# Where three short steps stand in a sketched attention and gated feed-forward kernel: two token differences and one set of key sums

## The chip, the core and the metric

The kernel runs on one core of a Trainium2 chip. The metric is the device time of one launch in microseconds. Five engines work side by side and meet through semaphores: TensorE (PE in the profile; its weight loads are listed as PEld), VectorE (DVE), ScalarE (ACT), GpSimd (POOL) and SyncE (SP), which here issues transfers. Each takes its instructions in the order of the program.

## The reference, cut to what matters

There are 4 batches, 4 heads, 1088 tokens and a head width of 32. Two 8 x 32 matrices sketch each query and key, and all products of the two sketches make 64 features:

```python
def phi(x):                       # 8 + 8 sketches -> 64 features
    a = np.einsum('rd,bhsd->bhsr', S1, x)
    b = np.einsum('rd,bhsd->bhsr', S2, x)
    return np.einsum('bhsi,bhsj->bhsij', a, b).reshape(*x.shape[:-1], 64)
q_p, k_p = phi(q), phi(k)
kv  = np.einsum('bhsf,bhsd->bhfd', k_p, v)
z   = np.sum(k_p, axis=2)
num = np.einsum('bhsf,bhfd->bhsd', q_p, kv)
den = np.einsum('bhsf,bhf->bhs', q_p, z)[..., None] + 1e-06
x   = (num / den)                 # then (batch, token, head*32): 4352 x 128
g   = x @ w_gate                  # 128 -> 1536
out = (g / (1 + np.exp(-g)) * (x @ w_val)) @ w_out    # 1536 -> 128
```

All is float32 at the interface.

## The kernel before, in words

**Tiling.** The tokens of batch 0 form three blocks of 384, 384 and 320 tokens, and all later tokens form seven blocks of 480, the last of 384 (`blocks`; `line` lists the later ones, so `line[0]` is the first later block and `line[2]` the third). The hidden width of 1536 is 12 chunks of 128. One unit of work is one chunk of one block: gate and value product, SiLU, product, and some units later the projection by `w_out` (`down`, L1045, matmul on L1066) into an accumulator.

**Split products.** Later blocks are computed by `cut_unit` (L965) from operands that are split in parts. For a block of tokens `x`, `cut_tokens` (L867) makes `x1`, the token values scaled by a factor just under one (ScalarE, L875), `x0 = x - x1` (L876) and, in a second step of the generator, the token difference `xd = x1 - 4096 x0` (VectorE, L880). The weights have parts `w1`, `wb`, `wd` likewise. A unit's first matmul (L974) multiplies `wd` by `xd`; ScalarE copies it, scaled, to `sums` (L978); two more matmuls (L984, L985) multiply `w1` by `x1` and `wb` by `x0`, and VectorE adds them into `sums` (L986), which frees the bank of these two. GpSimd then makes the hidden values (L997). Up to step 19 only the value product is split and the gate product is a plain one (L976); from step 20 on both are. A bank is one of eight in PSUM; each product takes the bank that has been left alone longest.

**Attention.** The attention of batches 1 to 3 is the generator `attentions` (L608). It is advanced a part at a time between the units (`parts_of`, L1230), and at a part marked "pe" it stops until `group` (L1237) lets it go on, at steps 4, 6, 20, 22 and 40. For a batch: transposes of the keys; their sketches (`key_products`, L343, matmuls on L347, in two pieces that go to two banks; copies on ScalarE, L583); the features `phk` in four products on VectorE (`features`, L702, instruction on L370); sums of these over the nine groups of tokens in five instructions on GpSimd (`feature_sums`, L536, L540), whose result is `zs`; then, in `values` (L709), 36 value products (`key_values`, L377, matmuls on L381) and 4 key-sum products of `zs` with ones (L713), both into one bank, `kv`. `fold` (L590) folds the key sums into the third set of sketch weights, `spread_out` (L718) turns `kv` and spreads it by small transfers, and `query_step` (L737) makes the query features, beginning with a product `dot` (L741) and a sum `den` (L744). `numerators` (L766) multiplies the two and writes the tokens of the batch, `xT`.

**Order.** The scheduler is set to keep the order written out. Around the change it is this. After batch 0's units a loop (L1323) runs the projections that remain, three at a time. Once `numerators(1, ...)` has been issued (`begun`), the same loop starts `cut_tokens(HEAD, nc.vector)` for the first later block, one step of the generator in each pass, with parts of attention between. Then comes the main loop over 84 units (`y`). At the end of its step `y`, after the parts of attention, it takes the steps of other blocks' `cut_tokens` that `token_steps` (L1342) names for `y`; GpSimd makes `x0` there. The third later block begins at `y` = 24.

Of the kernel before, what the change touches and what calls it, by code (L numbers as in the profile page):

```python
# [19 lines left out]
def kernel(  # L20
# [28 lines left out]
    nc = tc.nc  # L49
# [7 lines left out]
    NC = (NX + 3) // 4  # L57
    F = R * R
    NCH = Dff // P
# [38 lines left out]
    def touch(*which):  # L98
        for i in which:
            clock[0] += 1  # L100
            used[i] = clock[0]

    def hold(*tags):
        for t in tags:
            held.update((place[t], place[t] + 1) if t in "ab" else (place[t],))

    def release(*tags):
        for t in tags:
            banks = (place[t], place[t] + 1) if t in "ab" else (place[t],)
            held.difference_update(banks)  # L110
            touch(*banks)
# [19 lines left out]
    def wide(tag):  # L131
        i = place[tag]
        touch(i, i + 1)
        return PS[:, i : i + 2, :]
# [160 lines left out]
    def run(*gens):  # L295
        for g in gens:
            for _ in g:
                pass
# [78 lines left out]
    def key_values(kv, phk, c0, c1, order=range(NC)):  # L377

        for c in range(c0, c1):
            for h in range(H):  # L380
                nc.tensor.matmul(  # L381
                    kv[32 * h : 32 * h + 32, 0:F],
                    vld[:, h, c, :],
                    phk[:, c, h, :, :].rearrange("p i j -> p (i j)"),
                    start=(c == order[0]),
                    stop=(c == order[-1]),
                )
# [172 lines left out]
    def turn_keys(b):  # L560

        for c in kpieces:
            turn_k(*c)
            if c[1] == NC and b + 1 < B:
                load_k(b + 1)
            yield

    def turn_queries(b):

        for x0, x1 in ((0, 4 * kpieces[0][1]), (4 * kpieces[0][1], 4 * NC)):  # L570
            nc.vector.transpose(out=qT[:, x0:x1, :], in_=qld[:, x0:x1, :])
            if x1 == 4 * NC and b + 1 < B:
                load_q(b + 1)
            yield
# [15 lines left out]
    def fold(kv):  # L590

        t = apool.tile([P, R, R], FP32, tag="fold", name="fold")
        w = apool.tile([P, R], FP32, tag="w", name="w")
        nc.vector.tensor_tensor(
            out=t[:], in0=kv[:, F : 2 * F].rearrange("p (i j) -> p i j", j=R),
            in1=sq[:, 0, :, :], op=ALU.mult,
        )
        nc.vector.tensor_reduce(
            out=w[:], in_=t[:].rearrange("p i j -> p j i"), axis=AX.X, op=ALU.add
        )  # L600
        nc.vector.tensor_tensor(
            out=s123[:, :, 2, :],
            in0=w[:].unsqueeze(1).to_broadcast([P, 2 * H, R]),
            in1=own2[:].unsqueeze(2).to_broadcast([P, 2 * H, R]),
            op=ALU.mult,
        )

    def attentions():  # L608

        yield from turn_keys(1)
        yield from turn_queries(1)
        hold("a")
        kp = wide("a")
        for i, c in enumerate(kpieces):
            key_products(kp[:, i, :], *c)
        ka = apool.tile([P, NC * H, R], FP32, tag="kas", name="kas")

        def sketch(ps, i):  # L620
            c0, c1 = kpieces[i]
            return ps[:, i, 0 : 64 * (c1 - c0)].rearrange("p (x t r) -> p x t r", t=2, r=R)

        for i, (c0, c1) in enumerate(kpieces):
            nc.scalar.copy(ka[:, H * c0 : H * c1, :], sketch(kp, i)[:, :, 0, :])
        phk = apool.tile([P, NC, H, R, R], FP32, tag="phk", name="phk")
        for n, (i, c0, c1) in enumerate(((0, 0, 3), (0, 3, 5), (1, 5, 7), (1, 7, 9))):
            first = H * (c0 - kpieces[i][0])
            kb = sketch(kp, i)[:, first : first + H * (c1 - c0), 1, :]
            key_features(phk, (ka[:, H * c0 : H * c1, :], kb), c0, c1)  # L630
            if n == 3:
                release("a")
            if n % 3 != 1:
                yield
        zs, sums = feature_sums(phk)
        for f in sums:
            f()
        yield from turn_keys(2)
        kvz = wide("a")
        values(kvz[:, 0, :], phk, zs)  # L640
        kab, kcopies = sketched(wide("b"), key_products, 2, "kab2")
        fold(kvz[:, 0, :])
        spread = spread_out(1, kvz[:, 0, :])
        hold("a", "b")
        yield
        qab, copies = sketched(wide("a"), query_sketches, 3, "qab")
        run_copies(copies, 2)
        yield
        run_copies(kcopies, 2)
        release("a", "b")  # L650
        for n, _ in enumerate(query_step(1, qab)):
            if n % 2 == 1:
                yield
        yield
        yield
        numerators(1, spread)
        yield "first"

        phk = apool.tile([P, NC, H, R, R], FP32, tag="phk", name="phk")
        yield from features(phk, kab)  # L660
        zs, sums = feature_sums(phk)
        for f in sums:
            f()
        yield from turn_keys(3)
        yield from turn_queries(2)
        for b in (2, 3):
            yield "pe"
            if b == 3:
                numerators(2, spread)
            hold("a")  # L670
            kv = bank()
            kv_bank = [max(used, key=used.get)]
            release("a")
            values(kv, phk, zs)
            if b == 2:
                kab, copies = sketched(wide("a"), key_products, 2, "kab2")
                run_copies(copies, 2)
            fold(kv)
            spread = spread_out(b, kv)
            touch(*kv_bank)  # L680
            yield
            yield "pe"
            qab, copies = sketched(wide("b"), query_sketches, 3, "qab")
            run_copies(copies, 2)
            yield
            if b == 2:
                yield from turn_queries(3)
                phk = late[:, NL - 6 :, :].rearrange("p s (n h i j) -> p (s n) h i j", h=1, i=R, j=R)
                phk = phk.rearrange("p (c h) o i j -> p c (h o) i j", h=H)
                yield from features(phk, kab)  # L690
                zs, sums = feature_sums(phk)
            yield from beside(query_step(b, qab), sums)
        yield "pe"
        numerators(3, spread)
        yield

    def run_copies(copies, n):
        for f, *args in copies[:n]:
            f(*args)
        del copies[:n]  # L700
# [5 lines left out]
            if n % 3 != 1:  # L706
                yield

    def values(kv, phk, zs):  # L709

        key_values(kv[:, 0:F], phk, 0, NC)
        for h in range(H):
            nc.tensor.matmul(  # L713
                kv[32 * h : 32 * h + 32, F : 2 * F], ones[:], zs[:, F * h : F * h + F],
                start=True, stop=True,
            )
# [80 lines left out]
    HEAD = len(steps)  # L797
# [69 lines left out]
    def cut_tokens(i, engine=nc.gpsimd):  # L867

        t0, n = blocks[i]
        x = xT[:, t0 : t0 + n]  # L870
        x1, x0, xd = x_parts[i] = [
            apool.tile([P, WB], F32R, tag=tag, name=name, bufs=2)
            for tag, name in (("qb", "x1"), ("dT", "x0"), ("rd", "xd"))
        ]
        nc.scalar.activation(x1[:, 0:n], x, AF.Copy, scale=CUT)  # L875
        engine.tensor_tensor(  # L876
            out=x0[:, 0:n], in0=x, in1=whole(x1[:, 0:n]), op=ALU.subtract
        )
        yield
        nc.vector.scalar_tensor_tensor(  # L880
            out=xd[:, 0:n], in0=whole(x0[:, 0:n]), scalar=-BETA, in1=whole(x1[:, 0:n]),
            op0=ALU.mult, op1=ALU.add,
        )
# [297 lines left out]
    phk = apool.tile([P, NC, H, R, R], FP32, tag="phk", name="phk")  # L1181
# [11 lines left out]
    kvz = [apool.tile([P, P], FP32, name=x) for x in ("kvz0", "kvz1")]  # L1193
    nc.scalar.copy(zq[:], kz)
    kv = bank("acc")[:, 0:F]
# [32 lines left out]
    begun = [False]  # L1228
# [93 lines left out]
    x_steps = None  # L1322
    while todo:  # L1323
        for _ in range(min(3, len(todo))):
            down()
        if begun[0]:
            x_steps = x_steps or cut_tokens(HEAD, nc.vector)
            next(x_steps, None)
        parts_of(1 + (begun[0] and len(todo) > 2))
    while not begun[0]:  # L1330
        parts_of(1)
# [10 lines left out]
    token_steps = {}  # L1342
    for m, i in enumerate(line[1:], 1):
        gen = cut_tokens(i)
        for at in {1: (3, 8), 2: (20, 22), 3: (27, 32), 4: (40, 42)}.get(m, (NCH * m - 10, NCH * m - 9)):
            token_steps.setdefault(at, []).append(gen)
    oldest[0] = True
    hold("acc")
# [71 lines left out]
```

## Time and profile before

| What | Value |
|---|---|
| Time, median of 3 runs | 285.72 us (285.48 to 285.97) |
| Time of the profiled execution | 285.77 us |
| Span in its profile | 283.9 us |
| TensorE busy | 276.6 us, 97% |
| VectorE busy | 226.4 us, 80% |
| GpSimd busy | 181.9 us, 64% |
| ScalarE busy | 177.2 us, 62% |
| Feature products on VectorE, 128x512 (L370) | 0.67 us at 121.61, 1.76 us at 93.27 |
| `xd` on VectorE (L880), 7 times | 0.65 us least, 1.01 median, 1.33 most |
| Products on VectorE's L986, 128x480 | 0.61 to 0.66 us |
| Key-sum products (L713), 4 for a batch | 8 records of 0.22 us, pipelined: 0.29 us in all |

A busy share is a mean over the whole span. The chain of work that ended last follows the span back from its last instruction, at each step to what released it; a time on the chain is one that the kernel's end depends on. In the timeline a row is: start, duration, engine, line and operation, output and inputs, and in brackets how long the engine had been idle and what ended that. A float32 matmul is listed as two records, and records of pipelined matmuls overlap, so that the spacing of their starts or ends, and not their durations, gives TensorE's pace.

### The profile page before, as it was taken

The page shows a single profiled execution, that of the slowest core. Times are in us where ns is not written, and L with a number is a line of the kernel's source. Part 1 is how long each engine was busy: PE and PEld are TensorE (multiplying, and loading weights), DVE is VectorE, ACT ScalarE, POOL GpSimd, SP SyncE. Part 2 cuts the span into 40 slices and gives each one's busy share as a digit, 9 for nine tenths or more (in the row PEclk, how much of TensorE's full clock was granted, in tenths as well). Part 3 has the DMA queues.
Part 4 walks back from the last instruction along what each step waited for, and adds up shares of the span by engine and source line. Part 5 has one row for each costly group of instructions (what it writes and reads, how often), then busy time and mean ns, then how long its engine had stood idle before and what let it go on. Part 6 is the DMA issues. An engine that isn't in the chain of part 4 may idle for free.

```text
span 283.9 us, 5606 instructions
## 1 busy us (share of the span) xinstructions
PE 276.6 (97%) x2132; PEld 191.8 (68%) x2132; DVE 226.4 (80%) x327; ACT 177.2 (62%) x322; POOL 181.9 (64%) x176
## 2 busy tenths in 40 slices
PE   7899999999999999999999999999999999999994
PEld 6645565666656566555576677657777787778984
DVE  3997987976495995999648898749999999999741
ACT  2468565633401766655367776867988888887850
POOL 3314432279500796589935787759989899998660
PEclk9999999999999999999999999999999999999999
DMA  6573194222231123000200020001000200010021
GB/s 192 159 225 95 43 281 153 81 78 81 54 70 28 27 87 88 2 0 6 32 16 0 0 36 2 0 2 22 13 0 1 37 0 1 9 28 1 1 34 30
DMA packets 26139, 14.30 MB, mean 50 GB/s; under 512 B 19840, under 2 KB 24192, under 8 KB 26112
## 3 DMA queue, kind: packets, MB, share of 16 engines
q1 hardware_dynamic: 25456, 13.84, 18.8%
q8 instruction: 17, 0.28, 0.4%
q10 hardware_dynamic: 656, 0.10, 0.2%
q14 instruction: 10, 0.08, 0.1%
HBM read 11.41 MB, written 2.23 MB: 48 GB/s over the span
## 4 chain that ended last, share of the span: by engine, by line
PE 89%; DVE 5%; ACT 2%; DMA 2%; issue 1%; SPq 0%; DVEq 0%; ACTq 0%
PE PS L1066 24%; PE PS L1021 16%; PE PS L974 11%; PE PS L984 10%; PE PS L985 10%; PE PS L976 5%; PE PS L776 2%; PE PS L335 2%; PE PS L347 2%; DMA kld<-in_k_dram 2%; PE PS L1061 1%; PE PS L381 1%; PE PS L1058 1%; PE PS L1060 1%; DVE sum L986 1%
## 5 line engine op out<-in xcount | busy, mean ns | idle before, releaser
L997 POOL TENSOR_TENSOR hbuf<-sg,sum 128x480 f32<-128x480 f32 (+1 forms) x83 | 105.5, 1277 | 32.1 <-ACT sg L992 24.6
L986 DVE SCALAR_TENSOR_TENSOR sum<-PS,sum 128x960 f32<-128x960 f32 (+2 forms) x83 | 83.1, 1002 | 21.4 <-ACT sum L978 15.2
L978 ACT ACTIVATE sum<-PS 128x960 f32<-128x960 f32 (+2 forms) x83 | 70.8, 853 | 36.4 <-PE PS L974 35.4
L1066 PE MATMUL PS<-hbuf,wo 128*128 128x480 f32 (+3 forms) x142 | 57.5, 505 | 0.0
L974 PE MATMUL PS<-xd,gphq 128*128 128x480 f32 (+1 forms) x63 | 38.5, 612 | 0.5 <-DVE xd L880 0.5
L984 PE MATMUL PS<-x,w 128*128 128x480 f32 (+1 forms) x83 | 38.5, 464 | 0.0
L992 ACT ACTIVATE sg<-sum 128x480 f32<-128x480 f32 (+1 forms) x63 | 36.6, 582 | 1.6 <-DVE sum L986 1.3
L974 PE MATMUL PS<-xd,wd 128*128 128x480 f32 (+1 forms) x83 | 35.8, 432 | 0.5 <-DVE xd L880 0.5
L1066 PEld LDWEIGHTS PS<-hbuf,wo 128*128 128x128 f32 x142 | 26.6, 189 | 8.4 <-issue 0.9
L985 PE MATMUL PS<-x,wb 128*128 128x480 f32 (+1 forms) x83 | 31.2, 376 | 0.0
L1021 PE MATMUL PS<-xT,wg 128*128 128x384 f32 (+1 forms) x74 | 29.5, 480 | 0.0
L1021 PE MATMUL PS<-xT,wv 128*128 128x384 f32 (+1 forms) x74 | 28.8, 471 | 0.2 <-DVE wv L279 0.2
L1025 ACT ACTIVATE sg<-PS 128x384 f32<-128x384 f32 (+1 forms) x31 | 14.3, 466 | 21.4 <-PE PS L1021 19.6
L974 PEld LDWEIGHTS PS<-xd,wd 128*128 128x128 f32 x83 | 15.7, 189 | 12.1 <-issue 10.7
L984 PE MATMUL PS<-x,graw 128*128 128x480 f32 (+1 forms) x63 | 23.5, 374 | 0.2 <-ACT xT L793 0.2
L985 PE MATMUL PS<-x,graw 128*128 128x480 f32 (+1 forms) x63 | 23.3, 370 | 0.0
L1066 PE MATMUL PS<-hbuf,scaled 128*128 128x480 f32 x42 | 20.3, 564 | 0.0
L1021 PEld LDWEIGHTS PS<-xT,wv 128*128 128x128 f32 x74 | 13.8, 190 | 9.1 <-DVE hbuf L1036 0.8
L974 PEld LDWEIGHTS PS<-xd,gphq 128*128 128x128 f32 x63 | 11.8, 188 | 11.7 <-issue 4.9
L1021 PEld LDWEIGHTS PS<-xT,wg 128*128 128x128 f32 x74 | 13.3, 190 | 9.3 <-issue 1.2
L984 PEld LDWEIGHTS PS<-x,w 128*128 128x128 f32 x83 | 15.6, 188 | 5.8 <-issue 3.6
L985 PEld LDWEIGHTS PS<-x,wb 128*128 128x128 f32 x83 | 15.6, 188 | 5.7 <-issue 4.3
(173 smaller groups left out, 474.4 us busy)
## 6 DMA issues: line engine op xcount, KB each, us to landing
kld<-in_k_dram SPq DMA_DIRECT2D x4, 544.0 KB, 4.5
vld<-in_v_dram SPq DMA_DIRECT2D x12, 144.0 KB, 5.2
qld<-in_q_dram SPq DMA_DIRECT2D x3, 544.0 KB, 3.3
raw<-in_moe_w_out_dram SPq DMA_DIRECT2D x4, 384.0 KB, 4.6
raw<-in_moe_w_gate_dram SPq DMA_DIRECT2D x3, 384.0 KB, 3.3
raw<-in_moe_w_val_dram SPq DMA_DIRECT2D x3, 384.0 KB, 3.2
out_dram<-o SPq DMA_DIRECT2D x16, 60.0 KB, 2.0
vld<-in_v_dram SPq DMA_DIRECT2D x4, 112.0 KB, 4.4
```

Source lines behind the costliest of these rows:

```text
L335: nc.tensor.matmul(ps[32 * a : 32 * a + 32, 96 * (c - c0) : 96 * (c - c0) + 96], qT[:, 4 * c + a, :], s123[:, a : a + H, :, :].rearrange(" ...
L974: nc.tensor.matmul(ds[:, k], wd, xd, start=True, stop=True)
L976: nc.tensor.matmul(g, wg[:, j, :], xT[:, t0 : t0 + n], start=True, stop=True)
L978: nc.scalar.activation(sums, ds, AF.Copy, scale=-1.0 / BETA)
L984: nc.tensor.matmul(ps[:, k], w1, x1, start=True, stop=False)
L985: nc.tensor.matmul(ps[:, k], wb, x0, start=False, stop=True)
L986: nc.vector.scalar_tensor_tensor(out=sums, in0=ps, scalar=1.0 + 1.0 / BETA, in1=sums, op0=ALU.mult, op1=ALU.add)
L992: nc.scalar.activation(sg, sums[:, 0] if both else g, AF.Silu)
L997: nc.gpsimd.tensor_tensor(out=hj[:, 0:n], in0=sg, in1=sums[:, len(ws) - 1], op=ALU.mult)
L1021: nc.tensor.matmul(o[:, 0:n], w[:, j, :], xT[:, t0 : t0 + n], start=True, stop=True)
L1025: nc.scalar.activation(sg[:, 0:n], g[:, 0:n], AF.Silu)
L1066: nc.tensor.matmul(acc[i][:, 0:n], w, hidden[i, j][:, 0:n], **sides)
```

## The change

Three things move; no instruction is added or taken away.

- `values` is taken apart. Its callers now call `key_values` and `value_sums` (the 4 key-sum products) themselves. In batch 1 the order stays the same. In batch 2 the key products for batch 3 and their copies are issued between the two. In batch 3 nothing stands between.
- In the loop of remaining projections, both steps of `cut_tokens(HEAD, nc.vector)` are issued in the first pass after `begun`, ahead of the parts of attention: on VectorE, `xd` follows `x0` directly, and the four feature products of batch 2 follow both. Before, three of the four stood between.
- For the third later block the second step of `cut_tokens` is issued at the end of step 21 and not 22: on VectorE, `xd` stands ahead of the sum of unit 22 and of `dot` and `den` of the query step of batch 2's attention, where it stood after them.

```diff
-        values(kvz[:, 0, :], phk, zs)
+        key_values(kvz[:, 0, 0:F], phk, 0, NC)
+        value_sums(kvz[:, 0, :], zs)
         kab, kcopies = sketched(wide("b"), key_products, 2, "kab2")
...
-            values(kv, phk, zs)
+            key_values(kv[:, 0:F], phk, 0, NC)
             if b == 2:
                 kab, copies = sketched(wide("a"), key_products, 2, "kab2")
                 run_copies(copies, 2)
+            value_sums(kv, zs)
             fold(kv)
...
-    def values(kv, phk, zs):
-
-        key_values(kv[:, 0:F], phk, 0, NC)
+    def value_sums(kv, zs):
+
         for h in range(H):
             nc.tensor.matmul(
                 kv[32 * h : 32 * h + 32, F : 2 * F], ones[:], zs[:, F * h : F * h + F],
...
-        if begun[0]:
-            x_steps = x_steps or cut_tokens(HEAD, nc.vector)
-            next(x_steps, None)
+        if begun[0] and not x_steps:
+            x_steps = cut_tokens(HEAD, nc.vector)
+            run(x_steps)
         parts_of(1 + (begun[0] and len(todo) > 2))
...
-        for at in {1: (3, 8), 2: (20, 22), 3: (27, 32), 4: (40, 42)}.get(m, (NCH * m - 10, NCH * m - 9)):
+        for at in {1: (3, 8), 2: (20, 21), 3: (27, 32), 4: (40, 42)}.get(m, (NCH * m - 10, NCH * m - 9)):
             token_steps.setdefault(at, []).append(gen)
```

## The prediction

> **What bounds the kernel now.** I read the page from the top and then went to three places in the trace. The busy row and the chain of work that ended last say whose kernel it is:
>
> ```profile
> PE 276.6 (97%) x2132; PEld 191.8 (68%) x2132; DVE 226.4 (80%) x327; ACT 177.2 (62%) x322; POOL 181.9 (64%) x176
> PE 89%; DVE 5%; ACT 2%; DMA 2%; issue 1%; SPq 0%; DVEq 0%; ACTq 0%
> ```
>
> TensorE carries 89% of the chain, at full granted clock in all 40 slices. Nothing in the edits takes work off TensorE, so all they can win is a hole in its stream. The lists of what waits for `xd` name two such holes (three records, of which the weight load and the matmul of the second are one event):
>
> ```profile
>   PEld PS L974: 1.3, 1
>   PE PS L974: 1.0, 2
> ```
>
> The chain in order of time shows the first hole at 93 us:
>
> ```profile
> 90.05 0.66 DVE x L876
> ...
> 91.49 1.29 DVE phk L370 x2
> 92.78 0.58 DVE xd L880
> 93.36 0.14 issue
> 93.49 0.46 PE PS L974
> ```
>
> `x0` of the first later block is done at 90.71, but three feature products stand between it and `xd`. TensorE's last projection (L1066) ends at 93.03; `xd` ends at 93.35.
>
> The timeline shows the second hole at 152 us:
>
> ```profile
> 151.23 0.96 PE L1066 MATMUL PS<-hbuf,wo 128*128 128x480 f32 x2
> 151.62 0.45 DVE L744 TENSOR_REDUCE den<-dot 128x36 f32<-128x288 f32 x1
> 152.00 0.65 DVE L880 SCALAR_TENSOR_TENSOR xd<-x,x 128x480 fp32r<-128x480 f32 x1
> 152.70 0.48 PE L974 MATMUL PS<-xd,gphq 128*128 128x480 f32 x1 [0.51 <-DVE xd L880]
> ```
>
> Between the holes the chain leaves TensorE from 94.8 to 101.6, for VectorE and ScalarE, and comes back at the key products, whose second half needs a bank that VectorE frees late:
>
> ```profile
> 99.72 1.26 DVE L865 TENSOR_TENSOR late<-wg,graw 128x384 f32<-128x384 f32 x1
> 100.90 0.65 DVE L986 SCALAR_TENSOR_TENSOR sum<-PS,sum 128x480 f32<-128x480 f32 x1
> 101.60 0.55 PEld L347 LDWEIGHTS PS<-s,kT 128*64 128x64 f32 x16 [0.21 <-DVE sum L986]
> ```
>
> From 101.6 to 148.4, and from 152.7 to 189, the chain is TensorE alone.
>
> **What the Trainium skill says.** "SBUF — State Buffer", section "Who interferes with whom": a VectorE instruction with two SBUF inputs and a GpSimd instruction that reads SBUF take one pair of ports by turns, and whichever comes second waits for the first to finish. The trace agrees: the 128x512 feature product took 0.67 us at 121.61, but 1.76 at 93.27, where GpSimd's 1.53 us sum (92.95 to 94.48) was running; it ended 0.55 after that sum. "PSUM — Partial Sum Buffer", section "Engine vs sequencer instructions": the queues of ScalarE, VectorE and GpSimdE are strict FIFO, and matmuls run in program order. The trace agrees where `xd`, ready to run at 90.7, waited for the products ahead of it. So order alone decides here.
>
> **Part 1, the attention of batch 1 (`values` split).** The order of instructions on TensorE is the same as before: 36 value products, 4 key-sum products, 18 key products. Cost nothing, because nothing moves.
>
> **Part 2, `xd` of the first later block right after `x0`.** One VectorE instruction of 0.65 us (L880) moves ahead of three products (0.95, 0.65, 0.65). `xd` then ends near 91.4, 1.6 us before TensorE is done with L1066. Where a matmul of L974 follows L1066 without a wait, it ends 0.21 after it (150.30 after 150.09, from 149.55 + 0.75 and 149.12 + 0.97). So the first L974 ends at 93.03 + 0.21 = 93.24, where it ended at 93.95: TensorE is 0.71 us earlier.
>
> What is late next: the third product ends at 93.43 and no longer at 92.78, and GpSimd's first sum waits for it. But the fourth product then follows at once, before GpSimd has started (it took 0.17 us from the product's end to the sum's start), so it should cost 0.65 and not 1.76; the sum waits for it to end at 94.0 and takes about 1.2 more, to 95.2, where before the second sum started at 95.11. GpSimd loses 0.1 us; the next to need it on TensorE is the key sums, below. VectorE reaches the transpose at 94.95 some 0.95 us earlier, and runs without a gap to 101.55 before, so its sum for the fourth unit, the one that frees the bank, ends near 100.6. Were the fourth product delayed again, VectorE would gain nothing: its work is the same in sum. Bounds of VectorE's gain: 0 and 1.5 (the late weight difference at 99.72, too, waited for GpSimd, 1.26 against 0.55 for the one at 104.62). I take 0.93.
>
> **Part 3, key sums behind the next keys' products (batch 2).** The 4 key-sum products cost TensorE 0.22 to 0.28 us of issue (100.44 to 100.72 on the weight side; the next matmul followed 0.23 after their start at 142.22). I take 0.23. Before, they stood ahead of the key products, whose first half (20 records, 0.66 us) reached the bank's wait near 101.40: the stall was 0.20. The key sums' input was ready at 99.38, before the first value product at 99.47, so no wait is removed as things stand; but with TensorE 0.71 earlier they would be reached at 99.8 and the input comes at about 99.5 to 100.1, so now the move may cover up to 0.3.
> With the move TensorE reaches the second half at 101.40 - 0.71 - 0.23 = 100.46. The bank comes at 101.60 - 0.93 = 100.67. Then 16 records and the 0.23 of key sums. The next unit stood at 102.21: it gains 0.93 - 0.23 = **0.70 us**. With VectorE's gain at 0 it loses 0.23; with 1.14 or more it gains 0.91. Behind the key sums stands the next unit on TensorE, and on VectorE the fold (L594), which waits for them: before at 102.39, held by VectorE's own queue; after, the key sums end near 101.4 and VectorE reaches the fold at about 101.5. No stall. The two copies of the sketches on ScalarE (L583) come earlier by 0.9.
> From there to 148.4 all is TensorE's and moves as a whole. No DMA is moved past anything: the orders of SP, GpSimd and ScalarE are the same as before.
>
> **Part 4, `xd` of the third later block one unit earlier (step 21, not 22).** VectorE had a hole there:
>
> ```profile
> 144.25 2.46 DVE L986 SCALAR_TENSOR_TENSOR sum<-PS,sum 128x960 f32<-128x960 f32 x2 [0.56 <-ACT sum L978]
> 149.51 1.16 DVE L986 SCALAR_TENSOR_TENSOR sum<-PS,sum 128x960 f32<-128x960 f32 x1 [2.80 <-ACT sum L978]
> ```
>
> Its input `x0` left GpSimd at 145.95, so `xd` runs at 146.71 and ends by 148.0 even if GpSimd's product (146.12 to 147.34) is in its way. It costs nothing: the hole of 2.80 us hides it; if the hole were gone it would push the next sum by 0.65 to 1.0. Without it behind `dot` and `den`, the first matmul of the block ends at 152.19 + 0.21 = 152.40 and not 153.18: **0.78 us**. Is there a wait under it? The sum of the unit before then ends at 153.2 (152.02 + 1.15) and TensorE wants its banks back at 154.56 - 0.78 = 153.78: a margin of 0.6. The bank that the block's first matmul needs was free at 150.67.
>
> **Sum.** 0.70 + 0.78 = 1.48 us off the profiled execution, which took 285.77 (span 283.9 and 1.87 around it): 284.29. The median of the runs shown is 285.72, 0.05 lower: **284.25 us**, 0.5% faster. What a measurement of this kernel can tell from no change is about 0.2%, 0.57 us.
>
> **Rivals.**
> (a) *The first gain is swallowed.* VectorE is the bound from 93.3 to 103.8 (its instructions stand end to end), the fourth product waits for GpSimd after all, and TensorE meets the bank's wait at 101.6 as before, now with 0.23 of key sums behind it. Net 0.78 - 0.23 = 0.55: 285.17. For it: the chain of before runs through VectorE there. Against it: the 1.1 us that VectorE lost was GpSimd's lock, and the order now gives VectorE the lock first.
> (b) *One of the two holes is filled by another wait* (at 152 the banks of the unit before, margin 0.6; or the queue of VectorE after 153). Then 0.7 to 0.8 remain: 285.0.
> (c) *The change does not do what it says*: both holes turn into waits for something else of the same length, and time stays at 285.7. Against it: at both places no other releaser is near.
> (d) *Slower.* GpSimd's chain of sums is late, and the key sums, now last before the next unit, hold TensorE. They are reached at 101.2. With 1.48 gained elsewhere the kernel is slower by 0.57 only if the sums end after 101.2 + 0.57 + 1.48 = 103.2, against 99.38 before. GpSimd's five sums would have to lose the ports three times over, at 1.1 us each; only one VectorE instruction with two SBUF inputs, the weight difference, meets them now. At 104.0 it would be 286.5.
>
> **How the numbers follow.** Main case 0.68, (a) 0.14, (b) 0.09, (c) 0.05, (d) 0.04. Half of (a) lies on each side of the bound: faster 0.68 + 0.09 + 0.07 = 0.84, same 0.07 + 0.05 = 0.12, slower 0.04. The main case's own range is 283.8 to 284.8 (part 3 at 0.91 or at 0.3, a quarter of a microsecond of scatter); with (b) and half of (a) it reaches 285.2. Low end 283.7, if VectorE gains 1.5 and later stages pick up a little too.
>
> **What would show it.** Right: the first L974 follows L1066 near 93.0 with no wait for `xd`; the fourth product is back at some 0.65 us and the first sum of GpSimd starts at 93.6; the second half of the key products starts near 100.7; `xd` stands at 146 in VectorE's hole and the wait of 0.51 at 152 is gone. Wrong: a fourth product of 1.7 us, a start of the second half at 101.6, a wait for GpSimd at L713, or a wait of L974 at 152 for another releaser.

## The result, and the profile after

The changed kernel takes 284.02 us in the median of 6 runs, against 285.71 before: a ratio of 0.9949, 95% interval 0.9927 to 0.9972, so 0.5% faster. One of its six runs took 285.59, at a granted clock of 0.994 where the others had 0.999 or 1.000; it hardly moves the median. Beside other runs on another occasion it was 283.86 against 285.53, ratio 0.9950 (0.9935 to 0.9965). The forecast was 284.25.

The profiled execution took 283.83 us with a span of 282.0, 1.9 less than the 283.9 of before. After the change most line numbers below the first edit are higher by one: the first matmul of a unit is L975 and not L974, `xd` is L881, VectorE's sum is L987, the projection L1067, the key sums L714.

From the page of the changed kernel, the span, the busy row and the chain by engine:

```profile
span 282.0 us, 5606 instructions
PE 275.8 (98%) x2132; PEld 191.7 (68%) x2132; DVE 226.1 (80%) x327; ACT 177.2 (63%) x322; POOL 181.8 (64%) x176
PE 94%; DVE 2%; DMA 2%; ACT 1%; issue 0%; SPq 0%
```

The instruction count is what it was, and the busy times are within 0.8 us of what they were. VectorE's share of the chain fell from 5% to 2%, TensorE's rose from 89% to 94%. What changed is who waits. The list of `xd` in the changed kernel (engine, operation, shortest, median and longest duration in ns, and under it those who waited) has nobody in it any more:

```profile
L881 DVE SCALAR_TENSOR_TENSOR xd<-x,x x7: 645/1214/1321, 90.5 to 237.6; 128x480 fp32r<-128x480 f32 x6, 128x384 fp32r<-128x384 f32 x1
its engine sat idle before it (us, times) until:
who waited for it (us, times):
```

VectorE's timeline around the first block in the changed kernel:

```profile
90.47 0.66 DVE L881 SCALAR_TENSOR_TENSOR xd<-x,x 128x480 fp32r<-128x480 f32 x1
91.04 2.75 DVE L370 TENSOR_TENSOR phk<-kab 128x768 f32<-128x768 f32 x4
93.71 0.51 DVE L1109 STREAM_TRANSPOSE o<-PS 128x320 f32<-128x320 f32 x1
...
98.48 0.52 DVE L866 TENSOR_TENSOR late<-wg,graw 128x384 f32<-128x384 f32 x1
98.91 0.65 DVE L987 SCALAR_TENSOR_TENSOR sum<-PS,sum 128x480 f32<-128x480 f32 x1
```

`xd` is done at 91.1. L866 is a step of splitting the gate weights, the weight difference of the prediction. The four feature products together take 2.75 us; before, three took 2.15 and the fourth 1.76 alone. The sum that frees the bank of the key products starts at 98.91 and not at 100.90. TensorE over the same stretch of the changed kernel:

```profile
98.50 1.21 PE L381 MATMUL PS<-phk,vld 128*32 128x64 f32 x72
99.64 1.27 PE L347 MATMUL PS<-s,kT 128*64 128x64 f32 x36
100.84 0.32 PE L714 MATMUL PS<-zs,ones 128*32 128x64 f32 x8
101.09 0.48 PE L975 MATMUL PS<-xd,wd 128*128 128x480 f32 x1
```

The 36 key-product records are one piece of 1.27 us; before they were broken by the wait for the bank and spanned 1.56. Around the third block, VectorE and TensorE in the timeline of the changed kernel:

```profile
145.49 1.24 DVE L881 SCALAR_TENSOR_TENSOR xd<-x,x 128x480 fp32r<-128x480 f32 x1
148.38 1.16 DVE L987 SCALAR_TENSOR_TENSOR sum<-PS,sum 128x960 f32<-128x960 f32 x1 [1.65 <-ACT sum L979]
...
150.09 0.97 PE L1067 MATMUL PS<-hbuf,wo 128*128 128x480 f32 x2
150.52 0.76 PE L975 MATMUL PS<-xd,gphq 128*128 128x480 f32 x1
```

`xd` stands in VectorE's hole (1.24 us, since GpSimd's product from 144.99 to 146.21 was in its way: `xd` ends 0.52 after that product) and 1.65 us of the hole are left. The block's first matmul starts 0.43 after the projection, as in the unit before it (148.42 after 147.99).

**Where the 1.9 us came from.** Comparing ends of the same instruction in the two traces: the first L974/L975 of the first later block ended at 93.95 and ends at 92.97, 0.98 earlier; but the stretch ahead of it, which is the same code in both, was already 0.28 earlier (the projection at 88.46 now stands at 88.18). That leaves 0.70. The first unit after the key products' matmuls gained 0.15 more (102.70 to 101.57, 1.13 in all). That number stands still to 149.55 against 148.42. Then the third block adds 0.77 (153.18 to 151.28, 1.90 in all), and 1.9 is what the spans differ by. So 0.28 lies ahead of the change, 0.85 is the first block and its bank, 0.77 the third block.

The 0.28 is most likely no effect of the change. It is there from the start: the kernel's first key products (L347), whose keys have to be loaded first, begin at 6.45 before and at 6.15 after, and no edit touches anything that runs so early. `x0` of the first later block started at 90.05 before, 89.77 after, and anywhere from 89.66 to 90.24 in the profiles of the runs below. The medians agree: the profiled execution of before lies 0.06 above its median and that of after 0.19 below, and of the 1.69 between the medians the two places take 1.62. One thing stays open: the three profiles without the first move (89.97 to 90.24) all have `x0` later than the eleven with it (89.66 to 89.95). A single profile of this kernel carries that much scatter, 0.6 us, by the time the first later block begins.

### The profile page after: what moved, and what is told of

Read it like the earlier page. It is cut to its first block, busy times and chain, and to the rows that moved or that the text cites. A ratio compares the mean times of both kernels' runs of the same rounds, so it can differ in the third digit from the quotient of the medians.

```text
span 282.0 us, 5606 instructions
## 1 busy us (share of the span) xinstructions
PE 275.8 (98%) x2132; PEld 191.7 (68%) x2132; DVE 226.1 (80%) x327; ACT 177.2 (63%) x322; POOL 181.8 (64%) x176
## 4 chain that ended last, share of the span: by engine, by line
PE 94%; DVE 2%; DMA 2%; ACT 1%; issue 0%; SPq 0%
PE PS L1067 26%; PE PS L1022 16%; PE PS L975 11%; PE PS L985 11%; PE PS L986 11%; PE PS L977 6%; PE PS L777 2%; PE PS L347 2%; PE PS L335 2%; PE PS L381 2%; DMA kld<-in_k_dram 2%; PE PS L1062 1%; PE PS L1059 1%; PE PS L1061 1%; PE PS L1095 1%; PE PS L490 1%
## 5 line engine op out<-in xcount | busy, mean ns | idle before, releaser
L987 DVE SCALAR_TENSOR_TENSOR sum<-PS,sum 128x960 f32<-128x960 f32 (+2 forms) x83 | 83.1, 1003 | 18.8 <-ACT sum L979 13.8
L1067 PE MATMUL PS<-hbuf,wo 128*128 128x480 f32 (+3 forms) x142 | 57.5, 505 | 0.0
L975 PE MATMUL PS<-xd,gphq 128*128 128x480 f32 (+1 forms) x63 | 38.8, 616 | 0.0
L975 PE MATMUL PS<-xd,wd 128*128 128x480 f32 (+1 forms) x83 | 36.0, 433 | 0.0
L1067 PEld LDWEIGHTS PS<-hbuf,wo 128*128 128x128 f32 x142 | 26.6, 189 | 8.4 <-issue 0.9
L975 PEld LDWEIGHTS PS<-xd,wd 128*128 128x128 f32 x83 | 15.7, 189 | 11.5 <-issue 10.0
L1067 PE MATMUL PS<-hbuf,scaled 128*128 128x480 f32 x42 | 20.3, 564 | 0.0
L977 PE MATMUL PS<-xT,wg 128*128 128x480 f32 x40 | 19.3, 564 | 0.0
```

Source lines behind the costliest of these rows:

```text
L975: nc.tensor.matmul(ds[:, k], wd, xd, start=True, stop=True)
L977: nc.tensor.matmul(g, wg[:, j, :], xT[:, t0 : t0 + n], start=True, stop=True)
L987: nc.vector.scalar_tensor_tensor(out=sums, in0=ps, scalar=1.0 + 1.0 / BETA, in1=sums, op0=ALU.mult, op1=ALU.add)
L1067: nc.tensor.matmul(acc[i][:, 0:n], w, hidden[i, j][:, 0:n], **sides)
```

## The experiments

Each was run beside the kernel before; the medians are of 5 to 22 runs. "Change" is the difference of medians to the kernel before in the same group of runs.

| Run | What it is | Median, us | Before, us | Change, us | Ratio, 95% interval |
|---|---|---|---|---|---|
| e1_first_xd | first block's `xd` alone | 284.72 | 285.60 | -0.88 | 0.9961 to 0.9981 |
| e2_third_xd | third block's `xd` alone | 284.89 | 285.60 | -0.71 | 0.9968 to 0.9989 |
| e3_sums | key sums alone | 285.84 | 285.60 | +0.24 | 0.9999 to 1.0016 |
| e4_both_xd | both `xd`, not the key sums | 283.79 | 285.60 | -1.81 | 0.9927 to 0.9951 |
| e5_fill_between | whole + product before the 4th | 285.59 | 285.48 | +0.11 | 0.9990 to 1.0010 |
| e6_fill_behind | whole + product behind the 4th | 285.29 | 285.48 | -0.19 | 0.9979 to 0.9999 |
| e7_late_ahead | late GpSimd, key sums ahead | 285.20 | 285.48 | -0.28 | 0.9979 to 0.9998 |
| e8_late_behind | late GpSimd, key sums behind | 284.10 | 285.48 | -1.38 | 0.9933 to 0.9964 |
| e9_turn_behind | whole + transpose behind the 4th | 283.85 | 285.53 | -1.68 | 0.9926 to 0.9952 |
| e10_turn_between | whole + transpose before the 4th | 285.44 | 285.53 | -0.09 | 0.9992 to 1.0008 |
| e11_whole_again | whole change | 283.86 | 285.53 | -1.67 | 0.9935 to 0.9965 |
| e12_both_xd_again | as e4_both_xd | 283.90 | 285.53 | -1.63 | 0.9933 to 0.9956 |

### Each part alone

The first two runs put the key sums back ahead of the key products and keep one of the two moves of `xd`:

```diff
 # e1_first_xd
-        for at in {1: (3, 8), 2: (20, 21), ...
+        for at in {1: (3, 8), 2: (20, 22), ...
 # e2_third_xd
-            x_steps = cut_tokens(HEAD, nc.vector)
-            run(x_steps)
+            x_steps = x_steps or cut_tokens(HEAD, nc.vector)
+            next(x_steps, None)
```

> Only the token difference of the first later block is moved; key sums and the third block's difference stand as before. If it closes the hole at 93 us and VectorE keeps its bank early (theory): 0.7 to 0.9 us under before, 284.9, with the fourth feature product (128x512, L370) near 0.65 us. If VectorE is the bound there and takes it back (rival a): within 0.2 of before, 285.7.

> Only the token difference of the third later block is moved to step 21. Theory: the wait of L974 at 152 us goes, 0.75 to 0.8 us under before, 284.95. Rival b (another wait under it): 0 to 0.3 under before, with another releaser named at that matmul.

The first gave 0.88, at the upper end of what was expected; the second 0.71, just under the 0.75 to 0.8 expected. In the trace of the first the wait at the third block stands as before, and in that of the second the wait of 0.46 for `xd` at the first block, so closing one hole leaves the other as it was. From TensorE's timeline of e1_first_xd:

```profile
151.74 0.48 PE L975 MATMUL PS<-xd,gphq 128*128 128x480 f32 x1 [0.51 <-DVE xd L881]
```

In e2_third_xd the fourth feature product took 1.76 us again, and the wait for the bank, 0.18 at the weight load (PEld), is there again.

The third run keeps the key sums' move alone.

> Only the key sums of batch 2 are moved behind the next keys' products. Theory: no wait is removed and 0.2 us of issue comes out from under the bank's wait at 101.6: 0 to 0.25 us over before, 285.9. Rival (the key sums were waiting for GpSimd or hiding a wait): faster than before by 0.3 or more.

It came out 0.24 slower, with an interval that just reaches no change. TensorE's timeline of e3_sums shows why:

```profile
100.81 0.80 PE L347 MATMUL PS<-s,kT 128*64 128x64 f32 x20
101.80 0.69 PE L347 MATMUL PS<-s,kT 128*64 128x64 f32 x16 [0.19 <-DVE sum L987]
102.41 0.32 PE L714 MATMUL PS<-zs,ones 128*32 128x64 f32 x8
102.66 0.48 PE L975 MATMUL PS<-xd,wd 128*128 128x480 f32 x1
```

The key products come to the bank's wait sooner and wait longer (0.33 at the weight load against 0.21 before), and the 0.25 us of key sums now lie behind the wait. Ahead of it they had used time in which TensorE could do nothing else. Against its own `x0` (0.19 later than before's) the next unit is 0.26 later than in the kernel before.

### Both differences without the key sums

```diff
             key_values(kv[:, 0:F], phk, 0, NC)
+            value_sums(kv, zs)
             if b == 2:
                 kab, copies = sketched(wide("a"), key_products, 2, "kab2")
                 run_copies(copies, 2)
-            value_sums(kv, zs)
             fold(kv)
```

> Both token differences moved, key sums ahead of the key products as before. Theory: as fast as the whole change within 0.15 us, 284.0 to 284.2, since the key sums' input comes at about 99.6, as TensorE reaches them; a wait for GpSimd at the key sums of at most 0.1. Rival (the move of the key sums is needed once TensorE is early): 0.3 or more slower than the whole change, with a wait for GpSimd at L714.

> The whole change, beside the next run on the same chip: 283.9 to 284.1.

> Both token differences, key sums ahead, as in the fourth run. Theory: TensorE reaches the key sums just as their input is done, and the order of key sums and key products changes nothing: within 0.1 us of the whole change. Rival (key sums ahead are better, since VectorE's fold no longer waits for them): 0.2 under it.

The run was repeated beside the whole change on one chip: 283.90 and 283.86. No difference. The two runs of this same kernel gave 1.81 and 1.63 under before, which shows what 0.2 us between groups of runs is worth; each move alone gave 0.88 and 0.71, 1.59 in sum. From the timelines of TensorE and GpSimd in e4_both_xd:

```profile
99.54 0.32 PE L714 MATMUL PS<-zs,ones 128*32 128x64 f32 x8
98.35 1.14 POOL L540 TENSOR_TENSOR zs<-zs,phk 128x256 f32<-128x256 f32 x1
```

TensorE starts the key sums 0.05 us after GpSimd's last sum ends (99.49), and 1.16 after the first value product (98.38) where it was 1.03 before (99.47 to 100.50). So they do wait for GpSimd, by about 0.1 as expected, though the profile lists no idle time there; e1_first_xd and e12_both_xd_again show the same. Behind the key products they do not wait, but then the key products start 1.14 after the first value product, as in every profile here in which they follow the value products directly (1.14 to 1.15). From the first value product to the next unit it is 2.61 us in e4_both_xd and 2.59 in the changed kernel. `fold` starts at 99.93 on VectorE and not at 101.22, but nothing waited for it, so that bought nothing. With the bank's wait gone, there is no covered place left for the key sums: they cost the same on either side. So the 0.24 that they cost alone is not to be added to the rest: -0.88, -0.71 and +0.24 make -1.35, and the whole gives -1.67.

### What the key sums' place is worth when GpSimd is late

One extra sum on GpSimd (128x512, into a part of the tile that is free by then) delays the input of the key sums; the only difference between the runs is the place of `value_sums`:

```diff
             lambda: add(s[:, 0:2, :], s[:, 0:2, :], s[:, 2:4, :]),
+            lambda: add(s[:, 2:4, :], rows[:, 0:2, :], rows[:, 4:6, :]),   # batch 2 only
             last,
```

> One more sum of 1.28 us on GpSimd ahead of the last two of batch 2 (into a part of the tile that is no longer needed), with both token differences moved and the key sums ahead of the next keys' products. Theory: the key sums wait for GpSimd until about 100.9, TensorE stands 1.2 us there and the kernel is 1.0 to 1.3 us slower than the changed one: 285.1 to 285.3.

> The same extra sum on GpSimd, with the key sums behind the next keys' products. Theory: TensorE reaches the key sums at about 100.8, when their input is nearly there: 0 to 0.2 us slower than the changed kernel, 284.0 to 284.2. So this order is worth about 1.1 us of lateness on GpSimd. Rival (late hidden values hold TensorE or ScalarE instead): 0.5 or more slower.

Both as expected: 285.20 and 284.10, so the order is worth 1.1 us once the input is about 1.4 us late (GpSimd's last sum ends at 100.91 and 100.95, and at 99.49 in e4_both_xd). TensorE's timeline of e7_late_ahead:

```profile
98.45 1.21 PE L381 MATMUL PS<-phk,vld 128*32 128x64 f32 x72
100.96 0.32 PE L713 MATMUL PS<-zs,ones 128*32 128x64 f32 x8 [1.30 <-POOL zs L540]
```

In e8_late_behind the same matmuls start at 101.00, 1.38 after the first key product where it is 1.20 in the changed kernel, so 0.2 us of wait is left. Waiting for GpSimd at the key sums is also the mechanism of rival (d), made real on a small scale.

### Is it the ports? Extra work before and behind the fourth product

The prediction rested on VectorE's fourth product coming first at the ports that VectorE and GpSimd share. To set that against plain work, one extra VectorE product was put once before and once behind it:

```diff
+    def filler(kab):
+        t = apool.tile([P, NC * H, R], FP32, tag="dot", name="filler")
+        nc.vector.tensor_tensor(out=t[:], in0=kab[:, 0, :, :], in1=kab[:, 1, :, :], op=ALU.mult)
...
+            if n == 3 and fill == "between":
+                filler(kab)
             key_features(phk, (kab[:, 0, x, :], kab[:, 1, x, :]), c0, c1)
+            if n == 3 and fill == "behind":
+                filler(kab)
```

> The changed kernel with one extra VectorE product of 0.41 us with two SBUF inputs (128x288, into a tile that nothing reads) between the third and the fourth feature product of batch 2. Theory (the ports go to whoever is first): GpSimd's first sum starts before the fourth product, which then waits for it and takes about 1.7 us; VectorE loses about 1.5 us, more than the 0.74 it is ahead of TensorE at the key products' bank, and the kernel is 0.5 to 0.8 us slower than the changed one, 284.6 to 284.8. Rival (the ports are no matter, only the work counts): 0.41 is hidden in the 0.74 and the time stays at 284.0.

> The same extra product behind the fourth feature product, as a control. Theory: the fourth product keeps 0.65 us; the extra one may itself wait for GpSimd's sum, or hold it up. If it gets in ahead of GpSimd, VectorE loses 0.41, all hidden: 284.0. If it waits for the sum it costs 1.5, as in the run with it between: 284.6 to 284.8. The rival says 284.0 either way.

Both lost far more than the 0.45 us of work that the extra product is in e5_fill_between: 285.59 and 285.29, where 284.6 to 284.8 was expected (for the second, in the case that the extra product waits). The direction was right and the size was not, and the control by itself did not separate anything, because the extra product behind the fourth was itself held. VectorE in e6_fill_behind:

```profile
93.89 1.54 DVE L706 TENSOR_TENSOR filler<-kab 128x288 f32<-128x288 f32 x1
```

The cause of the size stands in VectorE's timeline of e5_fill_between:

```profile
93.24 0.45 DVE L706 TENSOR_TENSOR filler<-kab 128x288 f32<-128x288 f32 x1
93.61 1.77 DVE L370 TENSOR_TENSOR phk<-kab 128x512 f32<-128x512 f32 x1
...
100.07 1.26 DVE L874 TENSOR_TENSOR late<-wg,graw 128x384 f32<-128x384 f32 x1
101.25 0.65 DVE L995 SCALAR_TENSOR_TENSOR sum<-PS,sum 128x480 f32<-128x480 f32 x1
```

Delayed once, VectorE reaches the weight difference so late that GpSimd has begun its first product for the hidden values (99.70), and is held a second time: 1.26 us against 0.52 in the changed kernel (1.04 in e6_fill_behind). The sum that frees the bank starts 2.2 us later than in the changed kernel, counted from `x0` of each.

A control that GpSimd does not hold up was still wanted: a transpose of the same data, which has one SBUF input. In the changed kernel the transposes of 94.15 and 95.42 take 0.80 and 0.69 us while GpSimd's first two sums run (93.37 to 96.20), no longer than their means over the kernel (0.83 and 0.70).

```diff
-        nc.vector.tensor_tensor(out=t[:], in0=kab[:, 0, :, :], in1=kab[:, 1, :, :], op=ALU.mult)
+        nc.vector.transpose(
+            out=t[:].rearrange("p (c a) r -> p c (a r)", a=4),
+            in_=kab[:, 0, :, :].rearrange("p (c a) r -> p c (a r)", a=4),
+        )
```

> The changed kernel with an extra VectorE transpose of about the same length (128x288, one SBUF input, into a tile that nothing reads) behind the fourth feature product. In this trace transposes on VectorE ran beside GpSimd's sums at their usual length. Theory (the ports): the transpose takes about 0.4 us and is not held, the fourth product stays at 0.65, VectorE loses 0.4 to 0.8 of its 0.74 us lead at the bank: 284.0 to 284.2. Rival (VectorE's extra work as such costs the 1.3 us of the two runs before): 285.3.

> The same transpose between the third and the fourth feature product, so that GpSimd's sum is first at the ports. Theory: the fourth product takes 1.7 us; VectorE, now 1.5 us later, meets GpSimd's first hidden product with its weight difference as well and loses 0.7 more; TensorE waits some 1.2 us at the second half of the key products: 285.4 to 285.6. Rival (the place is no matter): the same time as with the transpose behind.

The same instruction, one place apart: 283.85 behind, 285.44 before, the whole change being 283.86 on the same chip. VectorE in e9_turn_behind:

```profile
91.08 2.76 DVE L370 TENSOR_TENSOR phk<-kab 128x768 f32<-128x768 f32 x4
93.75 0.47 DVE L706 STREAM_TRANSPOSE filler<-kab 128x288 f32<-128x288 f32 x1
...
98.88 0.78 DVE L877 TENSOR_TENSOR late<-wg,graw 128x384 f32<-128x384 f32 x1
```

VectorE in e10_turn_between, and the weight load on TensorE that waits for it:

```profile
93.09 0.47 DVE L706 STREAM_TRANSPOSE filler<-kab 128x288 f32<-128x288 f32 x1
93.48 1.69 DVE L370 TENSOR_TENSOR phk<-kab 128x512 f32<-128x512 f32 x1
...
99.86 1.28 DVE L877 TENSOR_TENSOR late<-wg,graw 128x384 f32<-128x384 f32 x1
...
101.77 0.55 PEld L347 LDWEIGHTS PS<-s,kT 128*64 128x64 f32 x16 [1.32 <-DVE sum L998]
```

Behind, the work of 0.4 us vanishes in VectorE's lead at the bank. Before, GpSimd's sum gets its start at 93.34 while VectorE transposes, the fourth product loses 1.0 us to it, the weight difference 0.76, and with the transpose's own 0.4 VectorE's sum is 2.2 us late; TensorE waits 1.32 at the weight load, and the kernel takes 1.59 us more than with the transpose behind.

In e9_turn_behind the transpose stands where the extra product stood in e6_fill_behind. On as many elements, beside the same sum of GpSimd, the product with two SBUF inputs was held to 1.54 us and the transpose with one took 0.47. So the loss is not that of extra work: it depends on the kind of instruction that meets GpSimd's sum, and on which of the two is first.

In e10_turn_between `xd` is as early as in the changed kernel and the first unit does not wait for it, yet the gain is given back at the bank. So it is shown that `xd` early is not enough: no instruction may stand between the third and the fourth product that lets GpSimd start first. Before the change, `xd` itself was that instruction. What the fourth product ahead of a late `xd` would gain was not run.

## Why the prediction was right, point by point

**First block (part 2).** Worked out as 0.71, measured 0.70 (0.98 less the 0.28 that lies ahead). The fourth product fell back to its short time and VectorE's transpose came 0.96 earlier on that count (94.95 to 93.71, less 0.28), where 0.95 was forecast. GpSimd's first sum was released by the third product as forecast.

**The bank (part 3).** Forecast as 0.70 for the first unit after it, measured 0.85, and this is the term that was off. The step that failed was VectorE's gain at the bank: 0.93 was taken, with 1.5 as the upper bound, and it was 1.71 (100.90 to 98.91, less 0.28). The weight difference ran in 0.52 us, ahead of GpSimd's last sum, which took 1.15 and not 0.74; the 0.93 had left it at the 1.26 it took before. Nor did the bound of 1.5 follow from the prediction's own figures: 0.93 and the 0.71 between 1.26 and 0.55 make 1.64. That the second meeting with GpSimd would go VectorE's way was not worked out, so the size of its lead is luck (see the end). So VectorE's sum was done at 99.56, 0.74 before TensorE came to the bank near 100.30 (99.64 and the 0.66 that the first half took before), and TensorE, not VectorE, set the pace. The upper value given for that case was 0.91; the trace has 0.06 less, and the value products took 1.14 us to the next group where they took 1.03 before. That 0.11 comes with the new order: it is in every profile here in which the key products follow the value products directly, and was not in the sum.

**Key sums (part 3).** Priced at 0.23 of issue with nothing won as things stood: the run with this move alone lost 0.24, with the wait under it as worked out. That it may cover up to 0.3 us of lateness came to about 0.1 with the key sums ahead, and the 0.11 at the start of the key products takes it back.

**Third block (part 4).** Worked out as 0.78, measured 0.77 in the trace and 0.71 as a difference of medians in the run alone. The contended length of `xd` (1.24 us) and its cover (1.65 us left over) were much as worked out, and no other wait lay under it.

**The rivals.** (a), that VectorE takes the first gain back, did not happen, but e10_turn_between shows how near it was: one short transpose in the wrong place brings it about. Its price was about right: 0.55 net was forecast to remain and 0.09 remained, no more than noise; what lies between is the transpose's own time, for VectorE's sum at the bank starts 11.32 us after `x0` there and 10.85 before, 0.47 later. (b) and (c) fell: both holes closed with nothing under them. (d) needs GpSimd late by 3.8 us (103.2 against 99.38); about 1.4 us, made with the key sums ahead, cost some 1.4. Its last figure was added up wrongly: sums that end at 104.0 would hold TensorE for 2.8 us from 101.2, which less the 1.48 gained is 1.32 slower, 287.0 and not 286.5.

**The total.** 1.48 forecast, 1.67 to 1.69 measured between medians; the parts in the trace make 1.62.

## What to carry to other kernels

In a kernel whose VectorE and GpSimd both work from SBUF, ask of each VectorE instruction with two SBUF inputs which engine gets there first, and keep such instructions close together ahead of the event that releases GpSimd: here one transpose of 0.47 us in between cost 1.59 us, and the delay brought about a second meeting further on. A step that others wait for is worth placing directly behind its input where its engine has an idle stretch, as at the third block; the idle stretch is found in the list of idle times before that engine's next instruction. Work that stands ahead of a wait on an in-order engine can be free as long as the wait is there; moved behind it, it is paid for, here with 0.24 us in a run whose interval just reaches no change.

## What the runs showed that was not expected

A delay on VectorE grew on its way: 0.4 us put in at 93 us was 2.2 us at 101 us (0.4 of its own, 1.0 and 0.76 at two meetings with GpSimd). The other way round, the changed kernel gained 0.74 at the second meeting because it came sooner. There the two engines' records begin within 0.02 us of each other, GpSimd's first; VectorE's weight difference starts at 98.48 and takes its usual 0.52, and GpSimd's last sum takes 0.4 longer than before:

```profile
98.46 1.15 POOL L540 TENSOR_TENSOR zs<-zs,phk 128x256 f32<-128x256 f32 x1
```

This is no single event: in e1_first_xd, e4_both_xd, e11_whole_again and e12_both_xd_again GpSimd's record begins 0.01 to 0.04 us ahead of VectorE's, and each time VectorE takes 0.51 or 0.52 and GpSimd 1.13 to 1.16. In e9_turn_behind VectorE comes 0.38 after GpSimd, and there it is VectorE that is held (0.78 us) and GpSimd that takes 0.74. So at a difference of a few hundredths, which may be no more than the profile's own roughness, the start of a GpSimd record does not tell which engine has the ports.
